# Work on a finished memory and rounding of the next x: placed behind the last key tile of a segment instead of ahead of and in the key tiles

## The chip, the cores and the metric

One core of one Trainium2 chip. The time is the device time of one execution, in microseconds (us). Before the change it was 1409.4 us, the median of 3 runs (1407.93 to 1409.66).

## What is computed

Two attention layers over the same shapes (2048 tokens, width 576, 32 heads of 18), whose outputs are concatenated. A is attention with one key and value head for all query heads. B works in four segments of 512 tokens: causal attention within a segment, mixed by a gate with what the queries read from a memory that the segments ahead have filled:

```python
phi = lambda t: jnp.where(t > 0, t + 1.0, jnp.exp(t))
...
for s in range(N):
    qs, ks, vs = q[:, :, s], k[:, :, s], v[:, :, s]
    logits = jnp.einsum("bhqd,bhkd->bhqk", qs, ks) * scale + mask
    p = _softmax(logits, axis=-1)
    a_dot = jnp.einsum("bhqk,bhkd->bhqd", p, vs)
    pq = phi(qs)
    num = jnp.einsum("bhld,bhde->bhle", pq, M)
    den = jnp.einsum("bhld,bhd->bhl", pq, z)[..., None] + 1e-6
    a_mem = num / den
    o = g * a_mem + (1.0 - g) * a_dot
    outs.append(o)
    pk = phi(ks)
    M = M + jnp.einsum("bhld,bhle->bhde", pk, vs)
    z = z + jnp.einsum("bhld->bhd", pk)
```

Everything is float32. The kernel reaches that accuracy by splitting each operand into a rounded high part and a low part, so that one product becomes three.

## The kernel before

The program has two halves. The first, to about 286 us, projects the inputs: A in four chunks, then B segment by segment (`for s in range(NSEG)`). Then every engine reads a flag and branches on it (L627, L628), and behind the branch comes the attention phase with its own order of work, which the change does not touch.

**A segment of B** goes through these stages, in the order of the code:

- *Five key tiles* (`for t in range(5)`, L449 to L477). TensorE computes the tile of the projection into `pj` (14 matmuls, L253). VectorE takes its maximum `kmB` (L459), ScalarE rounds it into the high part of `qp` (L122), VectorE subtracts for the low part (L123), and the DMA queue of SyncE (SP) stores both (L127). Then phi: two steps on ScalarE (L397, L398) and one on VectorE (L400) make `kf` (in the fifth tile `qf`). With the next tile TensorE transposes `kf` (`natural`, L427) and VectorE copies the result to `pkN` (L428).
- *The next x.* In segments 1 and 2, each key tile also calls `nx[2](t)` (L468), that is `load_xk`: a DMA on SP brings a slice of the next segment's x into `xr`, which has three buffers (L196), VectorE rounds it to `xh` (L209) and subtracts for `xl` (L215, L217). In segment 0 this is called in the query tiles instead.
- *`from_memory(4)`* (L479). For segments 1 and 2 (`LATE_ASK`) it only stores `qf` (L438), and the memory is asked in the attention phase; for segment 3 it multiplies with `Mst` on TensorE at once.
- *Values and keys of the last head.* `values(i, 0)` (L503) for four blocks of tokens, each followed by a copy to `vch` (L505) and a store to `vB` from ScalarE's DMA queue (L508). The transposes of `kn` (L519) give VectorE the maximum `km31` (L522; it stands as `km` in the rows). It is multiplied with `sely` on TensorE (L533) into the PSUM bank `mm`, of which there is one. Then `values(i, 1)`.
- *Four query tiles* (L539 to L551), the bound `pu` on the logits, its store `shB` (L571), and in segment 3 the flag (L412) and then `values(i, 1)`.
- *The memory.* In segments 0 to 2 TensorE adds up phi(k) times v into `pm`, again in the bank `mm` (L586 to L598). VectorE masks it with `bands` (L601), adds it to `Mbd` (L608), copies seven pieces into `Mst` (L613), reduces `zc` (L614) and spreads it over `zst` (L616, five tiles). For segments 0 and 1 two DMAs store `Mst` and `zst` to `mzB` (L618, L619).

In segment 0, most of these operations are pinned: they keep the order of the code. In the other segments a scheduler orders each engine's instructions by when their operands are expected, so the order on an engine is not that of the code. `tc.issue_after(ins)` makes what is issued within it stand behind the instruction `ins` on that engine.

Of the kernel before, what the change touches and what calls it, by code (L numbers as in the profile page):

```python
# [14 lines left out]
ALU = mybir.AluOpType  # L15
AX = mybir.AxisListType
# [10 lines left out]
RT = [18 * h for h in HT]  # L27
H0 = [0, 7, 14, 21, 28]
FIRST = [(0, 1, 3, 4), (0, 1, 1)]
# [7 lines left out]
VW = DH + 1  # L37
# [24 lines left out]
LATE_ASK, ASK = (1, 2), 20  # L62
# [13 lines left out]
def attention_pair_kernel(ctx, tc, a_xT, a_w, a_wo, b_xT, b_w, b_wo, b_beta, ident_d, hmask_d, bmask_d, cmask_d, sel_d, zmask_d, selx_d, sely_d, out):  # L76
    nc = tc.nc
# [26 lines left out]
    mzB = dram("mzB", [128, len(LATE_ASK), 5, MZ], F32)  # L104
# [52 lines left out]
    with ExitStack() as ph:  # L157
# [18 lines left out]
        zmask = pw.tile([128, 5, 32], F32, name="zmask")  # L176
# [87 lines left out]
        for c in range(NCH):  # L264
            ready = {}
            if c == 0:
# [8 lines left out]
                nx = next_x(a_xT, 1)  # L275
# [18 lines left out]
            else:  # L294
                xh, xl = nx[:2]
                nx = next_x(a_xT, c + 1) if c < NCH - 1 else next_x(b_xT, 0)
                if c == 2:
                    wBl, wBh = (pw.tile([128, 5, 3 * D], F32R, name=n) for n in ("wBl", "wBh"))
            for t in TILES:
# [8 lines left out]
                R = RT[t]  # L308
# [22 lines left out]
                i = 5 * (c - 2) + TILES.index(t)  # L331
# [31 lines left out]
        for t in range(5):  # L363
            R = RT[t]
# [14 lines left out]
        Mbd = p2.tile([128, 5, 3, VW], F32, name="Mbd")  # L379
        mx = p2.tile([128, 5, 3, VW], F32, name="mx")  # L380
        Mst = p2.tile([128, 5, 7, DH], F32, name="Mst")
        zst = p2.tile([128, 5, 32], F32, name="zst")
        nc.gpsimd.memset(Mbd, 0.0)
        nc.gpsimd.memset(mx, 0.0)
        bands = p2.tile([128, 2, 3, VW], F32, name="bands")
# [8 lines left out]
        def phi(src, R, nm, bufs, hold=lambda ins: ins):  # L394

            e = p2.tile([128, C], F32, name="ph_e", bufs=2)
            hold(nc.scalar.activation(e[:R], src, AF.Relu, scale=-1.0))  # L397
            hold(nc.scalar.activation(e[:R], e[:R], AF.Exp, scale=-1.0))  # L398
            f = p2.tile([128, C], F32, name=nm, bufs=bufs)
            hold(nc.vector.scalar_tensor_tensor(f[:R], src, 0.0, e[:R], op0=ALU.max, op1=ALU.add))  # L400
            return f

        def loose_flag():
# [7 lines left out]
            nc.vector.tensor_scalar(fm2[:, 1:2], fm2[:, 0:1], float(BOUND_OK), None, op0=ALU.is_gt)  # L411
            nc.vector.tensor_copy(flag, fm2[:, 1:2])  # L412

        for s in range(NSEG):
            xh, xl = nx[:2]
            last = s == NSEG - 1
# [18 lines left out]
            def from_memory(t):  # L435
                R = RT[t]
                if s in LATE_ASK:
                    nc.sync.dma_start(qfB[s][:R, t], fs[t][:R])  # L438
                    return
                pn = ps.tile([128, C], F32, name="mm", bufs=1)  # L440
                nc.tensor.matmul(
                    pn[:R], Mst[:R, t].rearrange("p h d -> p (h d)")[:, :R], fs[t][:R], start=True, stop=True
                )
                nm = p2.tile([128, C], F32, name="nm", bufs=2)
                nc.vector.tensor_scalar(nm[:R], pn[:R], gt[:R, t : t + 1], None, op0=ALU.mult)
                nc.sync.dma_start(numB[s][126 * t : 126 * t + R], nm[:R])


            for t in range(5):  # L449
                if s == t == 0:  # L450
                    pj = ahead
                else:
                    pj = ps.tile([128, C], F32, name="pj", bufs=4)
                    proj(pj[:126], wBh, wBl, xh, xl, 630 + 126 * t if t < 4 else 504, 126)
                if t and not last:
                    natural(f, pkN[:, t - 1, :, 0:126], 0, 126)

                hold = pin if s == 0 else lambda ins: ins
                hold(nc.vector.tensor_reduce(kmB[:126, t : t + 1], pj[:126], axis=AX.X, op=ALU.max, apply_absolute_value=True))  # L459
                qp = split2(pt, pj[:126], 126, hold)  # L460
                if t < 4:
                    store_parts(qp, 0, 126, kB[s], 7 * t, 7)
                    hold(nc.vector.tensor_scalar(kbB[:126, t], zmask[:126, t], kmB[:126, t : t + 1], None, op0=ALU.mult))
                else:
                    store_parts(qp, 0, 72, qB[s], 28, 4)
                    store_parts(qp, 72, 54, kB[s], 28, 3)
                    magnitude(4, pj)
                if s and not last:  # L468
                    nx[2](t)
                if not last or t == 4:  # L470
                    f = phi(pj[:126], 126, "kf" if t < 4 else "qf", 2 if t < 4 else 5, hold)
                    if t == 4:
                        fs[4] = f
                if s == 0:
                    split_wpart(10 + t)
                    if t < 4:
                        load_wpart(11 + t)  # L477
            if s:
                from_memory(4)  # L479
            if s == 0:  # L480
                nc.vector.memset(gt, 0.0)
                for t, lo, hi, n in [(t, H0[t], H0[t] + HT[t], DH) for t in range(5)] + [(5, 0, 28, 4), (6, 28, 32, 32)]:
# [10 lines left out]
            def values(i, hf):  # L493
                pj = ps.tile([128, C], F32, name="pj", bufs=4)
                ops = []
                tk = slice(128 * i, 128 * i + 128)
                n = 288 if hf else 306
                vc = slice(1440, 1728) if hf else slice(1134, 1440)
                for k in range(4):
                    ops += [(xh[:, k, tk], wBh[:, k, vc]), (xl[:, k, tk], wBh[:, k, vc]), (xh[:, k, tk], wBl[:, k, vc])]  # L500
                ops += [(xh[:, 4, tk], wBh[:, 4, vc]), (xh[:, 4, tk], wBl[:, 4, vc])]
                for m, (x, w) in enumerate(ops):
                    nc.tensor.matmul(pj[:, :n], x, w, start=m == 0, stop=m == len(ops) - 1)  # L503
                hs = slice(16 * hf, 16 * hf + 16)
                nc.scalar.copy(vch[:, i, hs, 1:VW], pj[:, :288].rearrange("p (h d) -> p h d", d=DH))  # L505
                if not hf:
                    nc.scalar.copy(kn[:, i], pj[:, 288:306])
                nc.scalar.dma_start(  # L508
                    vB[s][128 * i : 128 * i + 128, 304 * hf : 304 * hf + 304], vch[:, i, hs].rearrange("p h d -> p (h d)")
                )  # L510

            values(0, 0)
            if not last:
                natural(fs[4], pkN[:, 4, :, 0:54], 72, 126)
            for i in range(1, 4):
                values(i, 0)
            tr = ps.tile([128, 4, 128], F32, name="tr", bufs=1)
            for i in range(4):
                nc.tensor.transpose(tr[:DH, i], kn[:, i], ident)  # L519
# [15 lines left out]
            if not last:  # L535
                for i in range(4):
                    values(i, 1)

            for t in range(4):  # L539
                pj = ps.tile([128, C], F32, name="pj", bufs=4)  # L540
# [44 lines left out]
            if s < NSEG - 1:  # L585
                pm = ps.tile([128, C], F32, name="mm", bufs=1)[:, : 5 * 3 * VW].rearrange("p (t m) -> p t m", t=5)  # L586
                for t in range(5):
                    for i in range(4):
                        for g in range(4 if t < 4 else 3):
                            rows = slice(32 * g, min(32 * g + 32, RT[t]))  # L590
                            h = H0[t] + FIRST[t == 4][g]
                            nc.tensor.matmul(
                                pm[rows, t],
                                pkN[:, t, i, rows],
                                vch[:, i, h : h + 3, :].rearrange("p h d -> p (h d)"),
                                start=i == 0,
                                stop=i == 3,
                            )  # L598
                new = mx if s else Mbd
                for n, (R, ts) in enumerate(((126, slice(0, 4)), (72, slice(4, 5)))):  # L600
                    nc.vector.tensor_tensor(  # L601
                        new[:R, ts].rearrange("p t h d -> p t (h d)"),
                        pm[:R, ts],
                        bands[:R, n : n + 1].rearrange("p t h d -> p t (h d)").to_broadcast([R, ts.stop - ts.start, 3 * VW]),
                        op=ALU.mult,
                    )
                if s:
                    nc.vector.tensor_tensor(Mbd[:126], Mbd[:126], mx[:126], op=ALU.add)  # L608
                for ts in (slice(0, 4), slice(4, 5)):
                    for g in range(4 if ts.start < 4 else 3):  # L610
                        rows = slice(32 * g, min(32 * g + 32, RT[ts.start]))
                        w = FIRST[ts.start == 4][g]
                        nc.vector.tensor_copy(Mst[rows, ts, w : w + 3], Mbd[rows, ts, :, 1:VW])  # L613
                nc.vector.tensor_reduce(zc[:126], Mbd[:126, :, :, 0], axis=AX.X, op=ALU.add)  # L614
                for t in range(5):
                    nc.vector.tensor_scalar(zst[: RT[t], t], zmask[: RT[t], t], zc[: RT[t], t : t + 1], None, op0=ALU.mult)  # L616
                if s + 1 in LATE_ASK:
                    nc.sync.dma_start(mzB[:, s, :, :126], Mst.rearrange("p t h d -> p t (h d)"))  # L618
                    nc.sync.dma_start(mzB[:, s, :, 126:], zst)  # L619
            if s == 0:  # L620
                pin(nc.scalar.activation(gt, gt, AF.Exp, scale=-1.0))
                pin(nc.vector.tensor_scalar(gt, gt, 1.0, None, op0=ALU.add))
# [677 lines left out]
```

## Time and profile before

| | |
|---|---|
| Median of 3 runs | 1409.4 us |
| The profiled execution | 1409.26 us, its span 1407.5 us |
| Busy: TensorE (PE), ScalarE (ACT), VectorE (DVE), GpSimd (POOL) | 98%, 85%, 74%, 17% of the span |
| Granted clock of TensorE, mean | 0.995 |
| The four segments of B and the branch | about 118 to 288 us |

A row of a timeline has the start and the duration in us, the engine, the line, the operation, out<-in and the shape; in brackets stands how long the engine was idle ahead of it and what ended that. The letter q behind an engine (SPq, ACTq) marks what its queue does itself: issuing a DMA, a wait, a branch. VectorE's operations overlap a little at their ends, so how long one holds the engine is read from one start to the next.

### The profile page before, as it was taken

What the parts mean: (1) busy time and instruction counts of PE and PEld (TensorE: products, weight loads), DVE (VectorE), ACT (ScalarE), POOL (GpSimd) and SP (SyncE); (2) the same over time, 40 slices, a digit from 0 to 9 for tenths busy, and PEclk for the clock granted to TensorE, in tenths of its full rate; (3) what the DMA queues carried; (4) which work ended last, traced back from release to release, by engine and by line L of the source; (5) the groups of instructions that cost most, each with busy time, mean ns of one, the idle gap of its engine ahead of it and who ended that gap; (6) DMA issues with size and microseconds to landing.
All of it is one profiled execution on the core that took longest, in us unless ns stands there. A gap on an engine that the chain in (4) does not pass through costs nothing.

```text
span 1407.5 us, 41225 instructions
## 1 busy us (share of the span) xinstructions
PE 1386.2 (98%) x17468; PEld 837.5 (60%) x17468; DVE 1045.7 (74%) x1544; ACT 1198.8 (85%) x1479; POOL 234.4 (17%) x335
## 2 busy tenths in 40 slices
PE   9999999989999999999999999999999999999998
PEld 6787888745544555555555555555555555555558
DVE  6656456467787778777878878776879778887883
ACT  4543434479999999999999999999999999999991
POOL 2441000003302310402110122113010220001002
PEclk9999999989999999999999999999999999999999
DMA  9866546567575445332312442333103321120022
GB/s 282 259 213 188 169 149 214 184 177 218 145 215 165 118 137 176 98 119 85 112 58 71 146 144 60 94 106 91 51 33 94 109 75 44 32 67 18 18 69 103
DMA packets 90726, 172.70 MB, mean 123 GB/s; under 512 B 14576, under 2 KB 22889, under 8 KB 90110
## 3 DMA queue, kind: packets, MB, share of 16 engines
q1 hardware_dynamic: 84122, 160.01, 37.0%
q0 software_dynamic: 1664, 4.78, 1.3%
q10 hardware_dynamic: 4752, 5.24, 1.1%
q8 instruction: 138, 2.26, 0.7%
q14 instruction: 50, 0.41, 0.1%
HBM read 99.32 MB, written 70.67 MB: 121 GB/s over the span
## 4 chain that ended last, share of the span: by engine, by line
PE 71%; ACT 4%; DVE 2%; issue 1%; DMA 1%; POOL 0%; SPq 0%; ACTq 0%
PE O L991 33%; PE E L943 21%; PE F L796 11%; ACT P L961 4%; PE E L951 3%; PE E L1201 2%; DVE W L958 1%; PE F L852 1%; DMA vseg<-vB 0%; DMA woA<-a_wo 0%; DVE sm L747 0%; PE F L1201 0%; PE O L1201 0%; DVE o L857 0%; DVE oe L1000 0%
## 5 line engine op out<-in xcount | busy, mean ns | idle before, releaser
L961 ACT ACTIVATE P<-E 128x1024 f32<-128x1024 f32 (+1 forms) x800 | 789.4, 1079 | 4.8 <-PE E L943 4.6
L958 DVE COPY W<-E 128x1024 f32<-128x1024 f32 (+2 forms) x416 | 453.7, 1091 | 142.5 <-PE E L943 83.6
L991 PE MATMUL O<-P,VA 128*32 128x256 f32 x7504 | 508.1, 380 | 0.0
L961 ACT ACTIVATE P<-W 128x1024 f32<-128x1024 f32 (+1 forms) x330 | 370.7, 1123 | 6.9 <-DVE W L958 6.5
L991 PEld LDWEIGHTS O<-P,VA 128*32 128x32 f32 x7504 | 259.0, 110 | 139.1 <-issue 6.4
L943 PE MATMUL E<-stA,kstA 56*128 56x512 f32 x1920 | 317.0, 430 | 2.8 <-DVE W L958 1.9
L943 PEld LDWEIGHTS E<-stA,kstA 56*128 56x128 f32 x1920 | 154.6, 184 | 160.4 <-issue 93.0
L966 POOL TENSOR_SCALAR_AFFINE_SELECT P<-P 128x256 f32<-128x256 f32 (+1 forms) x192 | 95.0, 495 | 418.6 <-ACT P L961 380.6
L780 POOL TENSOR_TENSOR o<-o,rb 126x512 f32<-126x512 f32 (+1 forms) x55 | 72.8, 1350 | 488.6 <-DVE PD L926 328.9
L796 PE MATMUL F<-woB,o 126*32 126x192 f32 (+1 forms) x1920 | 126.6, 338 | 0.0
L991 PE MATMUL O<-PD,VA 128*32 128x256 f32 x688 | 88.9, 379 | 0.0
L796 PEld LDWEIGHTS F<-woB,o 126*32 126x32 f32 (+1 forms) x1920 | 38.6, 108 | 74.5 <-issue 68.7
L991 PE MATMUL O<-P,vseg 128*32 128x256 f32 (+2 forms) x1536 | 81.5, 344 | 0.1
L919 DVE TENSOR_SCALAR PD<-E 128x512 uint32<-128x512 f32 x86 | 59.4, 691 | 28.0 <-PE E L943 26.4
L1000 DVE COPY oe<-O 128x512 f32<-128x512 f32 x64 | 44.3, 692 | 41.7 <-PE O L991 40.8
L253 PE MATMUL pj<-xh,wBh 128*126 128x512 f32 x180 | 72.1, 401 | 0.0
L253 PE MATMUL pj<-xh,wBl 128*126 128x512 f32 x180 | 71.6, 398 | 0.0
L122 ACT CAST qp<-pj 126x512 fp32r<-126x512 f32 (+1 forms) x54 | 30.9, 584 | 44.2 <-DVE kmB L459 26.5
L123 DVE TENSOR_TENSOR qp<-pj,qp 126x512 fp32r<-126x512 f32 (+1 forms) x54 | 36.8, 686 | 39.5 <-ACT qp L122 39.3
L796 PE MATMUL F<-woA,o 126*32 126x192 f32 (+1 forms) x960 | 63.9, 338 | 0.0
L951 PE MATMUL E<-stB 56*128 56x256 f32 (+3 forms) x512 | 61.5, 347 | 2.1 <-ACT P L961 1.3
L991 PEld LDWEIGHTS O<-P,vseg 128*32 128x32 f32 x1536 | 48.8, 109 | 24.5 <-issue 1.9
(198 smaller groups left out, 1571.7 us busy)
## 6 DMA issues: line engine op xcount, KB each, us to landing
stB<-kB SPq DMA_DIRECT2D x96, 144.0 KB
stB<-qB SPq DMA_DIRECT2D x32, 288.0 KB
stA<-qA SPq DMA_DIRECT2D x30, 288.0 KB
oA<-oe SPq DMA_DIRECT2D x32, 256.0 KB
oB<-oe SPq DMA_DIRECT2D x32, 256.0 KB
qA<-qp SPq DMA_DIRECT2D x16, 504.0 KB
kB<-qp SPq DMA_DIRECT2D x16, 504.0 KB
qB<-qp SPq DMA_DIRECT2D x16, 504.0 KB
```

The source lines that it names most:

```text
L123: hold(nc.vector.tensor_tensor(qp[:R, 1, :n], src, qp[:R, 0, :n].bitcast(F32), op=ALU.subtract))
L253: nc.tensor.matmul(dst, w[:, c0 : c0 + M], x, start=i == 0, stop=i == len(ops) - 1)
L780: ins = tc.keep_in_program_order(nc.gpsimd.tensor_tensor(dst, a, b, op=op))
L796: nc.tensor.matmul(dst[32 * j : 32 * j + 32], parts[ab, c][: RT[t], t, r0 : r0 + 32], wo[ab][: RT[t], t, c0 : c0 + n], start=start, stop=stop,
L919: v.tensor_scalar(y, e, EXP_A, EXP_B, op0=ALU.mult, op1=ALU.add)
L943: nc.tensor.matmul(e[:, j], kstA[rows, 128 * kt : 128 * kt + 128], st[rows, h, :], start=True, stop=True)
L951: nc.tensor.matmul(e[:, j, c0 : c0 + 512 - 128 * k], st[rows, 4 + h, ks], st[rows, h, 128 * k :], start=True, stop=True)
L958: gate.append(nc.vector.tensor_copy(src[:, hs, :n], e[:, hs, :n]))
L961: nc.scalar.activation(p[:, hs, :n], src[:, hs, :n], AF.Exp, scale=SCALE)
L966: nc.gpsimd.affine_select(diag, diag, pattern=[[0, 2], [0, m], [1, 128]], base=0, channel_multiplier=-1, compare_op=ALU.is_ge, fill=0.0)
L991: nc.tensor.matmul(o[32 * j : 32 * j + 32, q0 : q0 + n], v, p[:, j % 2, p0 : p0 + n], start=m == hf == 0, stop=last and hf == 1,)
L1000: nc.vector.tensor_copy(osb, o)
```

## The change

The VectorE work on a finished memory (L601 to L619) becomes a function `collect`, which is called in the next segment, behind its five key tiles and after the last phi on VectorE. `from_memory(4)` moves behind the values of the first half. The calls that round the next x leave the key tiles: three stand among `values(1..3, 0)`, two among `values(0..1, 1)`.

```diff
-            hold(nc.vector.scalar_tensor_tensor(f[:R], src, 0.0, e[:R], op0=ALU.max, op1=ALU.add))
+            summed[:] = [hold(nc.vector.scalar_tensor_tensor(f[:R], src, 0.0, e[:R], op0=ALU.max, op1=ALU.add))]
             return f
...
+        rest, summed = [], []
         for s in range(NSEG):
...
-                if s and not last:
-                    nx[2](t)
                 if not last or t == 4:
...
             if s:
-                from_memory(4)
+                with tc.issue_after(summed[0].ins):
+                    rest.pop()()
...
             for i in range(1, 4):
+                if s and not last:
+                    nx[2](i - 1)
                 values(i, 0)
+            if s:
+                from_memory(4)
             tr = ps.tile([128, 4, 128], F32, name="tr", bufs=1)
...
                 for i in range(4):
                     values(i, 1)
+                    if s and i < 2:
+                        nx[2](3 + i)
...
-                new = mx if s else Mbd
...
+                def collect(s=s, pm=pm):
+                    new = mx if s else Mbd
...
+                    if s + 1 in LATE_ASK:
+                        nc.sync.dma_start(mzB[:, s, :, :126], Mst.rearrange("p t h d -> p t (h d)"))
+                        nc.sync.dma_start(mzB[:, s, :, 126:], zst)
+
+                rest.append(collect)
```

What the scheduler makes of it, at three places. First VectorE at the first key tile of segment 1, before (line numbers behind L400 shift by up to 9 between the two programs):

```order
L135 TENSOR_TENSOR shp<-sht,shp 128x512
L601 TENSOR_TENSOR Mbd<-mm,bands 126x228
L601 TENSOR_TENSOR Mbd<-mm,bands 72x57
L613 COPY Mst<-Mbd 32x4x54 x3
L613 COPY Mst<-Mbd 30x4x54
L613 COPY Mst<-Mbd 32x54 x2
L613 COPY Mst<-Mbd 8x54
L614 TENSOR_REDUCE zc<-Mbd 126x5
L459 TENSOR_REDUCE kmB<-pj 126x1
L616 TENSOR_SCALAR zst<-zmask,zc 126x32 x4
L616 TENSOR_SCALAR zst<-zmask,zc 72x32
```

and the same place now:

```order
L135 TENSOR_TENSOR shp<-sht,shp 128x512
L631 TENSOR_SCALAR gt<-gt 128x7
L209 CAST xh<-xr 128x512
L632 RECIPROCAL gt<-gt 128x7
L215 TENSOR_TENSOR xl<-xr,xh 128x512
L633 TENSOR_SCALAR omg<-gt 128x7
L209 CAST xh<-xr 128x512
L460 TENSOR_REDUCE kmB<-pj 126x1
L215 TENSOR_TENSOR xl<-xr,xh 128x512
L464 TENSOR_SCALAR kbB<-zmask,kmB 126x32
L123 TENSOR_TENSOR qp<-pj,qp 126x512
L209 CAST xh<-xr 128x512
```

The work on the memory has left this place, and the rounding of the next x (L209, L215), which stood behind the tile's `qp` before, now stands ahead of and behind `kmB`. In segment 2 it is the same: of L134, L135 and the rows between them and `kmB`, L601, L608, L613 and L614 have gone, and a cast and a subtraction of x more stand there, with one more cast right behind `kmB`.

Second, VectorE in segment 2 from the last phi to the maximum over `kn`, before:

```order
L400 SCALAR_TENSOR_TENSOR qf<-pj,ph_e 126x512
L209 CAST xh<-xr 128x512
L215 TENSOR_TENSOR xl<-xr,xh 128x512
L428 COPY pkN<-tr 128x4x54
L522 TENSOR_REDUCE km_2257<-tr 18x1
L534 TENSOR_SCALAR kbB<-zmask,mm 72x32
```

and now:

```order
L400 SCALAR_TENSOR_TENSOR qf<-pj,ph_e 126x512
L608 TENSOR_TENSOR mx<-mm,bands 126x228
L608 TENSOR_TENSOR mx<-mm,bands 72x57
L615 TENSOR_TENSOR Mbd<-Mbd,mx 126x285
L429 COPY pkN<-tr 128x4x54
L620 COPY Mst<-Mbd 32x4x54 x3
L620 COPY Mst<-Mbd 30x4x54
L620 COPY Mst<-Mbd 32x54 x2
L620 COPY Mst<-Mbd 8x54
L621 TENSOR_REDUCE zc<-Mbd 126x5
L526 TENSOR_REDUCE km_2248<-tr 18x1
```

The work on the memory stands here, ahead of the maximum `km`, and the rounding of the next x that stood here has gone. On TensorE, the matmul that reads `km` stands two matmuls later than before, and the transposes of the segment's first `kf` four matmuls earlier.

Third, ScalarE at the end of segment 3, where the last values are copied and stored and the flag is read, before:

```order
L505 COPY vch<-pj 128x16x18
L508 DMA vB_76<-vch 128x304
L505 COPY vch<-pj 128x16x18
L508 DMA vB_76<-vch 128x304
L505 COPY vch<-pj 128x16x18
L627 TENSOR_LOAD flag
L628 COMPARE_AND_BRANCH
```

and now:

```order
L505 COPY vch<-pj 128x16x18
L508 DMA vB_76<-vch 128x304
L505 COPY vch<-pj 128x16x18
L508 DMA vB_76<-vch 128x304
L636 TENSOR_LOAD flag
L637 COMPARE_AND_BRANCH
```

The DMA of the last values stood behind the branch and stands ahead of it now. In segment 3, TensorE's matmuls with `Mst` stand up to 12 matmuls later. Behind the branch the order of no engine differs.

More of the change, by code (lines that the diff above doesn't have):

```diff
@@ L598, in attention_pair_kernel @@
                             )
-                new = mx if s else Mbd
[L600 to L619, printed above, removed]
+                def collect(s=s, pm=pm):
+                    new = mx if s else Mbd
+                    for n, (R, ts) in enumerate(((126, slice(0, 4)), (72, slice(4, 5)))):
+                        nc.vector.tensor_tensor(
+                            new[:R, ts].rearrange("p t h d -> p t (h d)"),
+                            pm[:R, ts],
+                            bands[:R, n : n + 1].rearrange("p t h d -> p t (h d)").to_broadcast([R, ts.stop - ts.start, 3 * VW]),
+                            op=ALU.mult,
+                        )
+                    if s:
+                        nc.vector.tensor_tensor(Mbd[:126], Mbd[:126], mx[:126], op=ALU.add)
+                    for ts in (slice(0, 4), slice(4, 5)):
+                        for g in range(4 if ts.start < 4 else 3):
+                            rows = slice(32 * g, min(32 * g + 32, RT[ts.start]))
+                            w = FIRST[ts.start == 4][g]
+                            nc.vector.tensor_copy(Mst[rows, ts, w : w + 3], Mbd[rows, ts, :, 1:VW])
+                    nc.vector.tensor_reduce(zc[:126], Mbd[:126, :, :, 0], axis=AX.X, op=ALU.add)
+                    for t in range(5):
+                        nc.vector.tensor_scalar(zst[: RT[t], t], zmask[: RT[t], t], zc[: RT[t], t : t + 1], None, op0=ALU.mult)
+                    if s + 1 in LATE_ASK:
+                        nc.sync.dma_start(mzB[:, s, :, :126], Mst.rearrange("p t h d -> p t (h d)"))
+                        nc.sync.dma_start(mzB[:, s, :, 126:], zst)
```

## The prediction

> **What bounds the kernel now.** I read four views in this order: the page's busy times and chain, a table of stretches, TensorE's timeline through the segments, and then VectorE's, ScalarE's and the DMA queue's rows around each idle time of TensorE. First the page (busy us and share of the span for each engine, then the chain that ended last), and the stretches (start and end, length, busy time of each engine, granted clock, DMA share, GB/s):
>
> ```profile
> PE 1386.2 (98%) x17468; PEld 837.5 (60%) x17468; DVE 1045.7 (74%) x1544; ACT 1198.8 (85%) x1479; POOL 234.4 (17%) x335
> PE 71%; ACT 4%; DVE 2%; issue 1%; DMA 1%; POOL 0%; SPq 0%; ACTq 0%
> 118.00:286.00 168.00, 165.12 (x1304) 136.35 (x1303) 93.09 (x205) 65.66 (x137) 1.05 (x3) 1.00 0.59 188
> 286.16:287.73 1.57, 0.00 (x0) 0.03 (x1) 0.00 (x0) 0.40 (x1) 0.00 (x0) 1.00 0.05 14
> ```
>
> TensorE is busy for 98% of the span and carries 71% of the chain. VectorE's 74% is therefore no measure of what lighter VectorE work is worth: only where TensorE waits for VectorE can this change give time back. The four segments of B's part that it touches lie in the stretch 118 to 286, and there TensorE is idle for 168.00 − 165.12 = 2.88 us in all. Its timeline (start, duration, engine, line, operation; in brackets the idle time before it and what ended it) shows where:
>
> ```profile
> 137.80 0.62 PE L427 MATMUL tr<-ident,kf 126*128 126x126 f32 x4 [1.77 <-DVE kf L400]
> 190.49 0.65 PE L427 MATMUL tr<-ident,kf 126*128 126x126 f32 x4 [0.97 <-DVE kf L400]
> 287.73 1.12 PE L943 MATMUL E<-st,kstA 56*128 56x512 f32 x4 [1.57 <-SPq L628]
> ```
>
> Twice, at the first key tile of segments 1 and 2, the transposes of `kf` wait for VectorE: 1.77 + 0.97 = 2.74 us, or 0.19% of the run. That is all that a lighter VectorE can win. The third wait, 1.57 us, is the branch on the flag behind segment 3. The order of the attention phase behind the branch is the same before and after on every engine, so the whole effect lies ahead of and at the branch. A measurement of this kernel can tell about 0.2% (2.8 us) from no change.
>
> **Segment 1, first key tile.** VectorE's rows before:
>
> ```profile
> 130.69 0.51 DVE L601 TENSOR_TENSOR Mbd<-mm,bands 126x228 f32<-126x228 f32 x2
> 131.54 1.74 DVE L613 COPY Mst<-Mbd 32x216 f32<-32x216 f32 x7 [0.34 <-DVE Mbd L601]
> 133.41 0.68 DVE L459 TENSOR_REDUCE kmB<-pj 126x1 f32<-126x512 f32 x1
> 134.00 0.81 DVE L616 TENSOR_SCALAR zst<-zmask,zc 126x32 f32<-126x32 f32 x5
> 135.71 0.75 DVE L209 CAST xh<-xr 128x512 fp32r<-128x512 f32 x2
> 136.38 0.68 DVE L215 TENSOR_TENSOR xl<-xr,xh 128x512 fp32r<-128x512 f32 x1
> 136.98 0.68 DVE L400 SCALAR_TENSOR_TENSOR kf<-pj,ph_e 126x512 f32<-126x512 f32 x1
> ```
>
> From starts to starts, an operation of 512 columns holds VectorE 0.6 us (133.41 to 134.00) and a cast 0.34 (135.71 to 136.38, two). The work on the memory stands ahead of the maximum `kmB` and takes 133.41 − 130.69 = 2.72 us; from `kmB` to the end of `kf` it is 136.98 + 0.68 − 133.41 = 4.25 us. The change takes the 2.72 us away. But the rounding of the next x does not leave the key tiles: in the order as built, two casts, a subtraction and three tiny operations on the gate have moved up ahead of `kmB`. They cost 2 × 0.34 + 0.6 + about 0.35 = 1.6 us, so `kmB` starts at 132.3 instead of 133.4 and **1.1 us** is won, if the second cast finds its x. That x is loaded by the first of these two DMAs; the other rows show how long such a load takes (issue on the DMA queue, then the cast that uses it):
>
> ```profile
> 128.68 1.75 SPq L196 DMA_DIRECT2D xr<-b_xT  x2
> 217.44 0.37 SPq L196 DMA_DIRECT2D xr<-b_xT  x1
> 222.28 0.42 DVE L209 CAST xh<-xr 128x512 fp32r<-128x512 f32 x1
> 56.38 1.24 SPq L196 DMA_DIRECT2D xr<-b_xT  x2
> 64.30 0.43 DVE L209 CAST xh<-xr 128x512 fp32r<-128x512 f32 x1 [2.15 <-DMA xr<-b_xT]
> ```
>
> At 222.28 the x was there without a wait, so its load took at most 4.8 us; at 64.30 the cast waited for a load issued 7.9 us before, in the busiest stretch. The cast is now due at 128.68 + 3.25. I take 3.6 us for the load, an estimate between a quiet transfer (1.84 us at most, a row further down) and the 4.8 us: a stall of 0.35, **−0.75 us** in all. The ends are −1.1 (in time) and +0.5 (4.8 us). What is moved behind the last key tile is covered:
>
> ```profile
> 152.64 0.62 PE L427 MATMUL tr<-ident,qf 126*128 126x126 f32 x4
> 156.70 0.27 PE L519 MATMUL tr<-ident,kn 128*18 128x128 f32 x1
> ```
>
> The last `qf` was done by 152.64; 2.72 us and five small operations (0.7) later it is 156.1, and the next that TensorE needs of VectorE, the maximum over `kn`, can't start before 156.97. Without that 0.9 us of cover the work would cost what it overhangs. The two stores to `mzB` go with it; the stores queued behind them on the DMA queue are read only in the attention phase. No instruction of POOL or of its queue is moved.
>
> **Segment 2, first key tile.** VectorE's rows before, and TensorE's last matmul ahead of its wait:
>
> ```profile
> 181.33 0.42 DVE L134 CAST shp<-sht 128x512 fp32r<-128x512 f32 x1
> 183.66 0.68 DVE L215 TENSOR_TENSOR xl<-xr,xh 128x512 fp32r<-128x512 f32 x1
> 184.26 1.73 DVE L613 COPY Mst<-Mbd 32x216 f32<-32x216 f32 x7
> 186.13 0.68 DVE L459 TENSOR_REDUCE kmB<-pj 126x1 f32<-126x512 f32 x1
> 188.21 0.42 DVE L209 CAST xh<-xr 128x512 fp32r<-128x512 f32 x1
> 189.75 0.68 DVE L400 SCALAR_TENSOR_TENSOR kf<-pj,ph_e 126x512 f32<-126x512 f32 x1
> 189.12 0.39 PE L253 MATMUL pj<-xl,wBh 128*126 128x512 f32 x1
> ```
>
> After, two casts (L134 and one of x) and four operations of 512 columns stand between 181.33 and `kmB`: 2 × 0.34 + 4 × 0.6 = 3.1 us, `kmB` at 184.4 instead of 186.1. Right behind it stands another cast of x, and the load of that x can only be issued when a subtraction has freed one of the three `xr` buffers, at 181.33 + 0.34 + 0.6 + 0.1 = 182.4. With 3.6 us for the load it lands at 186.0, while VectorE comes to the cast at 185.0: a stall of 1.0 us, with the first `kf` queued behind it. Walking on (cast, subtraction, low part, next `kmB`, then the two exponential steps on ScalarE) `kf` ends at 189.75, and the transposes could start at 189.85. But in TensorE's order they now stand 4 matmuls earlier (4 × 0.23 us), so TensorE comes there at 188.6: a wait of 1.27 us instead of 0.97, **+0.3 us**. With the x in time it would wait 0.3 (−0.7); with 4.8 us of load, 2.5 (+1.5).
>
> **Segment 2, maximum over kn.** Before, VectorE is idle when the transposes of `kn` arrive:
>
> ```profile
> 221.68 0.68 DVE L400 SCALAR_TENSOR_TENSOR qf<-pj,ph_e 126x512 f32<-126x512 f32 x1
> 222.50 0.62 PE L427 MATMUL tr<-ident,qf 126*128 126x126 f32 x4
> 224.52 0.68 DVE L522 TENSOR_REDUCE km<-tr 18x1 f32<-18x512 f32 x1 [0.81 <-PE tr L519]
> 225.33 0.28 PE L533 MATMUL mm<-km,sely 18*72 18x1 f32 x2
> ```
>
> After, the seven copies into `Mst` (1.77 us) and the reduction to `zc` come between. The last `qf` ends on VectorE at 222.3; two products, a sum, the copy of `pkN`, which waits until 223.35 for its transposes (one place later than the 222.50 of before), the seven copies and `zc` bring the reduction to 225.5 and its end to 226.2. TensorE comes to the matmul on `km` two matmuls later than before, at 225.85. **+0.4 us**, from nothing (if the copies come up earlier) to 0.8. In segment 3 the work on the last memory likewise stands behind the last `qf`, with the matmuls that read `Mst` 12 places later: +0.1, from 0 to 0.3, for in the order TensorE still has 31 matmuls of values to run.
>
> **The branch.** ScalarE's and the DMA queues' rows:
>
> ```profile
> 284.76 0.33 ACTq L508 DMA_DIRECT2D vB<-vch  x1
> 286.20 0.40 ACT L505 COPY vch<-pj 128x288 f32<-128x288 f32 x1 [1.47 <-PE pj L503]
> 287.43 0.33 ACTq L508 DMA_DIRECT2D vB<-vch  x1
> L628 SPq EVENT_SEMAPHORE  x8: 17/17/17, 287.0 to 287.5; - x8
> 203.69 0.33 ACTq L508 DMA_DIRECT2D vB<-vch  x1
> 205.53 0.38 SPq L619 DMA_DIRECT2D mzB<-zst  x1
> SPq L619 <- DMA vB<-vch: 13.7, 1, 13.7
> ```
>
> The SyncE side of the branch waits on eight semaphores, those of the DMA queues, between 287.0 and 287.5, and TensorE starts at 287.73. Before, the last of the value stores stood behind the branch (issued at 287.43), so the last to be waited for was the one issued at 284.76, done by 287.0: 2.24 us at most. Now the last store stands ahead of the branch. Its copy still ends at 286.60, it is issued at 286.63, and it has to land first. A store of the same kind on quiet queues took at most 205.53 − 203.69 = 1.84 us (in the last row the second store waits for the first). So it lands between 288.47 and 288.87, and the rest of the eight and the start of TensorE follow in 0.43 to 0.73 us: 288.9 to 289.6. That is +1.2 to +1.85; I take **+1.5 us**, the middle, since both rows are of this very store. TensorE is idle in all that time, as the row of the stretch 286.16 to 287.73 shows (0.00 busy), and nothing hides it.
>
> The Trainium skill, "DMA: Bandwidth & Descriptors", section "Anatomy of one DMA — SWDGE (gpsimd) path", gives a fixed part of about 2.0 us, mostly the receipt of the write, and bytes over 436 GB/s, for another kind of queue; for this store of 156 KB that is an estimate of 2.36 us. By it the branch would cost 1.7 to 2.0 us and the sum would be 0.3 us higher. The trace's 1.84 is below it, so I keep the rows.
>
> **The sum** is made against the profiled execution, 1409.26 us (span 1407.5), which is 0.14 us under the median of 1409.4: −0.75 + 0.3 + 0.4 + 0.1 + 1.5 = +1.55, so **1410.8 us**.
>
> **The rivals.**
> - *The branch costs nothing* (chance 0.12): the last store may be covered by another wait of the eight, or the branch may not look at that queue. For it speaks that the eight semaphores take 0.5 us whatever is late. Against it, the last store comes 1.87 us behind the third. With both x in time: 1409.26 − 1.1 − 0.7 + 0.4 = 1407.9 us.
> - *Slower: the hoisted rounding stands in front of the key tile and waits for late x* (0.15). The place is the cast ahead of `kmB` in segment 1 and the cast behind it in segment 2. It decides from a load of more than 3.25 us and 2.6 us, and each tenth beyond is lost in full. Its price is a stall as at 64.30, 2.15 us, in each, in place of the 0.35 and 1.0 us of the forecast: (2.15 − 1.1) + (2.15 − 0.7) + 0.4 + 0.1 + 1.5 = +4.5, 1413.8 us. For it: the load of segment 2 is issued together with `shB` and the loads of `kstA`. Against it: only two casts of x waited in the whole run, both in the stage before.
> - *The change does not do what it says* (counted with the forecast): for the rounding this is already so in the order, and in the forecast. Were VectorE's gain nothing as well, it would be 1409.26 + 0.4 + 0.1 + 1.5 = 1411.3, within the forecast.
> - *The longer idle time at the branch costs clock* (0.12). The last rows:
>
> ```profile
> 288.50:289.00 0.50, 0.35 (x3) 0.00 (x0) 0.00 (x0) 0.36 (x1) 0.00 (x0) 0.70 0.52 172
> 289.00:298.00 9.00, 7.29 (x40) 3.37 (x41) 6.99 (x10) 7.75 (x9) 0.22 (x1) 0.50 0.51 118
> 298.00:299.00 1.00, 1.00 (x6) 0.34 (x4) 0.23 (x1) 0.65 (x1) 0.00 (x0) 0.53 0.63 145
> ```
>
> The granted clock is half from about 288.7 to 298.9, 10.2 us behind an idle time of 1.57. With 3.1 us idle it may stay low a third longer: 3.4 us at half speed lose 1.7, 1412.5 us. The Trainium skill, "TensorE: Matmul & The Clock Gate", section "Part 1: The HAM clock gate", tells of a free-running window of about 3.4 us, after an idle one of which the clock is halved, until a busy one. The 10.2 us are three such windows, which agrees; the halving after only 1.57 us of full idleness does not fit its wording closely.
>
> **How the numbers follow.** The forecast has 0.61. Its own terms reach from −1.1 − 0.7 + 0 + 0 + 1.2 = −0.6 to 0.5 + 1.5 + 0.8 + 0.3 + 1.85 = +4.95, with all five at one end, 1408.7 to 1414.2. The range that leaves out no more than 2 in 10 goes down to the first rival, with 0.3 us for the spread of the runs (1407.93 to 1409.66 before), and up to the second: 1407.6 to 1413.8. Faster by over 0.2% means below 1406.6, which is below every case (the whole 2.74 us would give 1406.5): 0.04. Slower by over 0.2% means above 1412.2: the second rival, half of the clock's, and the upper tail of the forecast, 0.22. Within: 0.74.
>
> **What would show it.** Right: TensorE's wait at the first `kf` of segment 1 falls from 1.77 to about 1.0; that of segment 2 stays between 0.3 and 2.5, released by VectorE behind a cast that itself waits for a DMA; a new wait of about 0.4 at the matmul on `km` of segment 2; the store of values issued before the branch, and the wait there about 3.1 us. Wrong: a wait at the branch still of 1.6 (first rival), idle time of 2 us at the casts (second), half clock for some 14 us (clock), or a difference of time within the attention phase, which I take as unchanged.

## The result and the profile after

The changed kernel takes 1414.17 us (median of 7 runs, 1411.61 to 1415.2) against 1408.68 before: a ratio of 1.0031, 95% interval 1.0022 to 1.0041. Run once more as an experiment, beside others, it took 1411.64 us (11 runs) against 1408.65: 1.0021, interval 1.0012 to 1.0030. By these ratios it is slower by 4.4 and 3.0 us, where 1.5 was forecast. The first medians are 5.5 us apart: four of the seven runs took 1414.2 to 1415.2 us and three 1411.6 to 1412.3, which is where the second measurement lies. The direction is the forecast one, but the size is two to three times as large, and beyond the 0.2% to which the forecast gave most of its chance. The second measurement lies well inside the range. The first lies at its upper end of 1413.8: 1.0031 times the 1409.26 from which the sum was made is 1413.6, and the median itself, 1414.17, is 0.4 above it. The profiled run took 1414.61 us, its span is 1412.9.

First the places at which the prediction expected something, on TensorE (idle time ahead and its cause in brackets):

```profile
139.33 0.62 PE L428 MATMUL tr<-ident,kf 126*128 126x126 f32 x4 [1.17 <-DVE kbB L464]
191.45 0.65 PE L428 MATMUL tr<-ident,kf 126*128 126x126 f32 x4 [1.25 <-DVE kf L400]
225.74 0.28 PE L537 MATMUL mm<-km,sely 18*72 18x1 f32 x2 [0.22 <-DVE km L526]
293.90 1.85 PE L952 MATMUL E<-st,kstA 56*128 56x512 f32 x6 [4.91 <-SPq L637]
```

The wait at the first `kf` of segment 1 fell from 1.77 to 1.17 us, that of segment 2 rose from 0.97 to 1.25, the matmul on `km` waits newly for 0.22, and the wait at the branch rose from 1.57 to 4.91 us. The first two are close to the forecast (1.0, 1.27), the third is half of it (0.4); the fourth is not (3.1).

VectorE at the first key tiles of segments 1 and 2 shows why the gain is so small:

```profile
132.90 0.42 DVE L209 CAST xh<-xr 128x512 fp32r<-128x512 f32 x1
133.35 0.69 DVE L215 TENSOR_TENSOR xl<-xr,xh 128x512 fp32r<-128x512 f32 x1
134.51 0.43 DVE L209 CAST xh<-xr 128x512 fp32r<-128x512 f32 x1 [0.38 <-DMA xr<-b_xT]
134.85 0.68 DVE L460 TENSOR_REDUCE kmB<-pj 126x1 f32<-126x512 f32 x1
187.60 0.43 DVE L209 CAST xh<-xr 128x512 fp32r<-128x512 f32 x1 [0.79 <-DMA xr<-b_xT]
```

The rounding of the next x stands ahead of `kmB`, and VectorE, which waited for no load here before, waits for that of x: 0.38 us in segment 1 (forecast 0.35) and 0.79 in segment 2 (forecast 1.0).

To add up, the program is cut at five marks of TensorE's timeline: the start of the last memory matmul of segments 0, 1 and 2, the end of the last matmul of values, and the first matmul of the attention phase. us:

| run | segment 1 | segment 2 | segment 3 | wait at the branch | attention to the end |
|---|---|---|---|---|---|
| before | 52.82 | 51.76 | 54.29 | 1.57 | 1119.8 |
| changed, first profile | 52.27 | 52.61 | 54.68 | 4.91 | 1119.0 |
| changed, second profile | 52.00 | 52.54 | 54.69 | 4.20 | 1118.8 |

From the first profile: −0.55 + 0.85 + 0.39 + 3.34 − 0.8 = +3.2 us. Its span is 5.4 longer; the other 2.1 lie ahead of segment 1, nearly all in code that is the same. Of them 1.9 arise in the first 10 us:

```profile
6.13 1.17 PE L285 MATMUL pj<-xh,wAh 128*114 128x512 f32 x4 [0.58 <-DVE wAh L226]
```

```profile
6.57 2.02 PE L285 MATMUL pj<-xh,wAh 128*114 128x512 f32 x4 [1.00 <-DVE wAh L226]
```

The first row is of before, the second of the changed kernel: the same four matmuls took 1.17 and 2.02 us. The granted clock was full from 5.4 us on in the one run and from 10.2 in the other, and in the second profile of the changed kernel from 7.5. So about 1.4 us of this single run are the lower clock at its start, and 0.4 the longer wait in front of that row. The second profile, only 0.2 us late at segment 1, is the better witness: −0.82 + 0.78 + 0.40 + 2.63 − 0.95 + 0.2 = +2.2 us against the span of before.

### The profile page after: what moved, and what is told of

It reads as the page before. It is cut to its first block, busy times and chain, and to the rows that moved or that the text cites. A ratio compares the mean times of both kernels' runs of the same rounds, so it can differ in the third digit from the quotient of the medians.

```text
span 1412.9 us, 41220 instructions
## 1 busy us (share of the span) xinstructions
PE 1388.8 (98%) x17468; PEld 838.8 (59%) x17468; DVE 1044.5 (74%) x1544; ACT 1198.7 (85%) x1479; POOL 233.4 (17%) x335
## 4 chain that ended last, share of the span: by engine, by line
PE 70%; ACT 4%; DVE 2%; DMA 2%; issue 1%; SPq 0%; POOL 0%; ACTq 0%
PE O L1000 32%; PE E L952 20%; PE F L805 11%; ACT P L970 4%; PE E L960 3%; PE E L1210 2%; PE F L861 1%; DVE W L967 1%; DMA oB<-oe 1%; DMA vseg<-vB 0%; DVE sm L756 0%; DMA o<-oB 0%; DMA woA<-a_wo 0%; PE F L1210 0%; PE O L1210 0%
```

## The experiments

**Theory 1**: the loss is the wait at the branch, because the last store of values now stands ahead of ScalarE's read of the flag. **Theory 2**: it is the moved VectorE work itself, which delays segments 2 and 3. The first two kernels move one instruction each.

**The last store ahead of the flag, all else as before.** `stored` holds the last DMA to `vB`:

```diff
-    loose = nc.values_load(flag[0:1, 0:1], min_val=0, max_val=1)
+    with tc.issue_after(stored[0].ins):
+        loose = nc.values_load(flag[0:1, 0:1], min_val=0, max_val=1)
```

> The kernel before, with one instruction moved: ScalarE's last store of values stands ahead of its read of the flag instead of behind the branch; nothing else differs on any engine. Theory 1 (the store that the branch waits for is the larger part of the loss): the wait of TensorE at the branch rises from 1.57 us to between 3.1 and 4.9, and the time by 1.5 to 3.4 us (0.1 to 0.24%), the waits at the two first kf stay. Theory 2 (the loss is the moved VectorE work and TensorE's changed order in segments 2 and 3): no change within 0.5 us.

Measured: 1410.81 us (11 runs) against 1408.81, ratio 1.0015 (1.0006 to 1.0024). The segments are those of before to 0.2 us (52.81, 51.56, 54.29). TensorE's waits and the last store in the timeline, then the eight semaphores on SyncE (duration in ns, first and last start):

```profile
137.39 0.62 PE L428 MATMUL tr<-ident,kf 126*128 126x126 f32 x4 [1.78 <-DVE kf L400]
290.20 1.95 PE L945 MATMUL E<-st,kstA 56*128 56x512 f32 x6 [4.66 <-SPq L630]
286.00 0.33 ACTq L509 DMA_DIRECT2D vB<-vch  x1
```

```profile
L630 SPq EVENT_SEMAPHORE  x8: 17/17/17, 286.3 to 290.1; - x8
```

One store, issued as soon as its copy ends, costs 3.1 us at the branch. It accounts for the whole wait; theory 2 expected none of it. The time rises by 2.0 us, which is two thirds of the 3.0 that the changed kernel loses in its second measurement. But in the prediction the store was to cost 1.5, and it took from 286.00 to 289.60 to land, 3.6 us, not 2.2.

**The changed kernel, its last store on GpSimd's software queue**, which SyncE's side of the branch does not wait for:

```diff
-                nc.scalar.dma_start(
+                (nc.gpsimd if last and (i, hf) == (3, 1) else nc.scalar).dma_start(
```

> The changed kernel, with one instruction moved: the last store of values is issued on GpSimd's software queue, whose semaphores SyncE's side of the branch does not wait for. Theory 1: the wait of TensorE at the branch falls from 4.9 to about 1.6 us, and the time to about 0.7 us over before (0 to 1.5), that is 2 to 4 us under the changed kernel. Theory 2: the wait may fall, but the time stays 3 us or more over before.

Measured: 1409.5 us against 1408.81, ratio 1.0002 (0.9993 to 1.0011). No loss can be told from the spread any more, with segments 2 and 3 as long as in the changed kernel (52.73, 54.66). The wait fell to 2.66 us, not to 1.6: the third store, issued at 287.35, landed only at 290.68. The store `shB`, issued in front of it at 286.08, is about 1 us nearer to the branch than before, since the flag comes later in segment 3; that this is the cause was not tried by itself. The fetch described below is not: it runs from 290.02 to 291.30, and the last packets of this store pass in its first 0.2 us.

**One half of the change alone.** First the memory work alone, with `nx[2](t)` called in the key tiles again:

> The changed kernel with the rounding of the next x called in the key tiles as before; only the work on the memory and the store of the last query part stay moved. The engines' orders differ from the changed kernel in a few rows late in segment 2 only. Theory 1 (the store at the branch, which comes with the moved memory work): as the changed kernel, 2.5 to 5.5 us over before, wait at the branch 4 to 5 us. Theory 2, in the form that the moved calls of the rounding cost: within 1 us of before.

Measured: 1411.67 us against 1408.65, ratio 1.0020 (1.0011 to 1.0029), wait at the branch 4.68, segments 51.97, 52.82 and 54.72. This is the changed kernel in every part, to 0.3 us. Then the calls of the rounding alone:

> The kernel before with the calls of the rounding moved as in the change, and nothing else. In the order the work on the memory still stands ahead of the first kmB, and the last store of values stands behind the branch. Theory 1: within 1 us of before, waits of about 1.8 and 1.0 us at the two first kf and 1.6 at the branch. Theory 2: 2 us or more over before.

Measured: 1408.95 us, ratio 1.0003 (0.9994 to 1.0012), waits of 1.79 us at the first `kf` and 1.56 at the branch. So the half of the change that was to move the rounding does nothing that can be measured: the scheduler, which orders by readiness, puts it where VectorE has room, and it was the departure of the memory work that drew it ahead of `kmB`.

**The changed kernel again**, beside these two:

> The changed kernel once more, beside the others on one chip. Theory 1: 3 to 5 us over before, wait at the branch 4 to 5 us with a 16 KB fetch of instructions in it, of some 1.6 us, ahead of the last 8 rows of the last store. If that fetch is a chance of one profile, the wait is 3.1 us.

Measured: 1411.64 us, ratio 1.0021 (1.0012 to 1.0030), wait at the branch 4.20. The fetch of instructions that the expectation speaks of is there again: 1.03 us long, ahead of the end of the last store.

**What makes the store so late.** In the first profile of the changed kernel, the DMA traffic of two stretches, 290.2 to 292.2 and 291.4 to 293.3 (busy tenths of the 16 DMA engines in 40 slices; then, for each queue, packets, MB and share of the 16 engines). Queue q10 is ScalarE's, q8 fetches instructions:

```profile
DMA  0069989998632000000000000000000000010010
...
q10 hardware_dynamic: 141, 0.15, 22.6%
q8 instruction: 1, 0.02, 5.1%
```

```profile
DMA  0000000000001001020010010000000000000000
...
q10 hardware_dynamic: 9, 0.01, 2.8%
```

The store's packets pass by 290.9, and then one fetch of 16 KB holds one DMA engine: 5.1% of 16 engines over 2 us are 1.6 us. Only then do the last nine packets of the store come, eight rows of 1216 bytes and the signal, one after the other as from a single engine. (The profile does not name a packet's engine; that they share one is read from the times.) In the trace the fetch runs from 290.36 to 292.00 and the first of the nine starts at 291.99; in the experiment with one store moved, from 286.80 to 288.29 and at 288.28. In the other three profiles with the last store ahead of the branch on ScalarE's queue, and without the added matmuls that follow, the first of the nine starts within 0.02 us of the fetch's end, too. Fifteen of the store's sixteen signals were there at 291.41 (287.78), the last at 293.30 (289.60). The fetch starts 1.0 to 1.5 us behind TensorE's own branch in every profile; before, it ran at 287.40, when no store was waited for any more. The Trainium skill, "Runtime: NRT & Kernel Launch", section "Instruction fetch mechanics", has it that instructions come by DMA in pieces of 16 KiB and that a branch can force such a fetch; the size and the place agree.

If the fetch is the cause, later matmuls should make it faster. Ten unused matmuls of 128x288 (1.34 us) ahead of TensorE's read of the flag push the branch, and so the fetch, back:

```diff
+                if last and (i, hf) == (3, 1):
+                    pad = ps.tile([128, C], F32, name="mm", bufs=1)
+                    with tc.issue_after(end.ins):
+                        for m in range(10):
+                            padded[:] = [nc.tensor.matmul(pad[:, :n], *ops[m], start=m == 0, stop=m == 9)]
```

> The changed kernel with 10 more matmuls of 128x288 (1.3 us, their result is not used) on TensorE between the last values and its read of the flag; nothing else differs. Theory F (the 16 KB fetch of instructions, which starts 1.0 to 1.4 us behind TensorE's branch, holds one DMA engine and that engine's rows of the last store): the fetch moves 1.3 us back, the store lands whole within 2.3 us of its issue, and SyncE passes the branch 1 to 1.8 us earlier after that issue than in the changed kernel, so TensorE's idle time behind its last matmul falls from 4.2 to 4.9 to about 1.5 to 2 us and the time is 0.5 to 1.5 us under the changed kernel, in spite of more work. Theory S (the store takes 2.9 to 3.9 us by itself): the first matmul of the attention phase comes as long after the store's issue as before, and the time stays.

> The kernel before with the last store ahead of the flag (as in the first experiment) and the same 10 matmuls of 128x288 ahead of TensorE's read of the flag. Theory F: TensorE's idle time falls from 4.66 to about 1.5 to 2 us, and the first matmul of the attention phase comes 1 to 1.8 us earlier after the store's issue than in the first experiment; the time is 0.5 to 1.5 us under that one. Theory S: it comes as long after the store's issue as there, and the time stays.

Measured, on the kernel before with its store ahead of the flag:

```profile
286.46 0.33 ACTq L514 DMA_DIRECT2D vB<-vch  x1
289.09 1.27 PE L950 MATMUL E<-st,kstA 56*128 56x512 f32 x6 [1.77 <-SPq L635]
```

From the store's issue to the first matmul of the attention phase it is 2.63 us, where it was 290.20 − 286.00 = 4.20: 1.57 us less with 1.34 us more work. The store landed 2.03 us after its issue, and the fetch (288.96) came behind it. Idle time and added matmuls together are 3.11 us, 1.54 over the 1.57 of before. The time is 1409.43 us, ratio 1.0010 (1.0001 to 1.0019), against 1.0015 without the matmuls. On the changed kernel the same took the wait from 4.20 to 2.42 us, not to the expected 1.5 to 2, and the time to 1410.55, ratio 1.0014 (1.0005 to 1.0023) against 1.0021. The traces show theory F; the times lean its way, but their intervals overlap. In the padded changed kernel the store still took 2.7 us. An earlier fetch of 16 KB ran there from 284.04 to 285.28, and the last signal of the stores under way came 0.4 to 2.1 us after their others, as if one DMA engine were behind; that it was this fetch was not tried.

**The rounding really held behind the last phi**, as the change says:

```diff
                 if s and not last:
-                    nx[2](i - 1)
+                    with tc.issue_after(summed[0].ins):
+                        nx[2](i - 1)
...
                     if s and i < 2:
-                        nx[2](3 + i)
+                        with tc.issue_after(summed[0].ins):
+                            nx[2](3 + i)
```

> The changed kernel, with the rounding of the next x also issued behind the last phi of the key tiles (as the work on the memory is), so that it really leaves them. Theory 1: both waits of TensorE at the first kf are gone (up to 2.7 us), the loads of x are early enough, and the store at the branch still costs 1.5 to 3.4: the time is between 1.5 us under and 1.5 us over before. Theory 2: what stands behind the last phi delays the maximum over kn, the query tiles and the Mst matmuls further, new waits of over 1 us there, and the time is 4 us or more over before.

Measured: 1412.87 us, ratio 1.0026 (1.0016 to 1.0037). Theory 1 was wrong here, and theory 2 right. Both waits at the first `kf` are gone and segment 1 takes 50.94 us, but segment 2 takes 53.83 and segment 3 55.47. In segment 2 (VectorE's cast, then TensorE):

```profile
227.82 0.43 DVE L209 CAST xh<-xr 128x512 fp32r<-128x512 f32 x1 [2.48 <-DMA xr<-b_xT]
230.01 0.39 PE L574 MATMUL nd<-aq,kbB 126*32 126x512 bf16 x2 [2.31 <-ACT aq L434]
```

The cast of x waits for its load in front of the query tiles' work, as the second rival had it, only later in the segment, and behind it TensorE waits 2.31 us for ScalarE. The granted clock then is half from 230.86 to 234.27, across the end of segment 2, which it is at this place in no kernel without the long wait; TensorE is busy all that time, so about 1.7 us more are lost (an estimate: half of 3.41). With the last store on GpSimd's queue as well:

> The rounding held behind the last phi and the last store of values on GpSimd's software queue, together. Theory 1: 1 to 2.5 us under before (about 1406.5 to 1408), with no wait of TensorE at a first kf and about 1.6 us at the branch. Theory 2: still slower than before.

Measured: 1408.8 us, ratio 0.9999 (0.9990 to 1.0008); segments 50.97, 53.88 and 55.88, 2.67 at the branch. So neither theory came true: it is neither faster nor slower. Segment 1 wins 1.85 us, segments 2 and 3 lose 3.7 and the branch 1.1; in the profile, most of this comes back behind the branch, where the phase takes 1117.4 us instead of 1119.8 and the half clock lasts 6.83 us instead of 10.24. That part is not a gain that the placement was shown to bring.

**Placed by segment.** Before the change, VectorE is idle in segment 2 between the third and the fourth key tile (from 200 to 216 us it has one operation). So the last kernel holds both pieces of work behind the last phi in segment 1 and behind the third tile's in segment 2, and leaves the memory work ahead of segment 3, and segment 3's `from_memory(4)`, where they were (the lines for the latter are left out here):

```diff
+                    if t == (2 if s == 2 else 4):
+                        anchor[:] = summed
...
-            if s:
-                with tc.issue_after(summed[0].ins):
+            if rest:
+                with tc.issue_after(anchor[0].ins):
                     rest.pop()()
...
-                rest.append(collect)
+                if s == 2:
+                    collect()
+                else:
+                    rest.append(collect)
```

with `anchor` in place of `summed` for the rounding, too.

> Work on the memory and rounding held behind the last phi in segment 1, behind the phi of the third key tile in segment 2 (where VectorE idles 7 us before the fourth), and the memory work ahead of segment 3 as before; in the order the last store of values stands behind the branch again. Theory 1: both waits at the first kf gone, no new one over 0.6 us, 1.6 us at the branch: 1.5 to 2.7 us under before (1406 to 1407.5). Theory 2 (what stands behind a phi always meets another wait of the same size): within 1 us of before or slower.

Measured: 1405.9 us (11 runs, 1404.94 to 1407.05) against 1408.65, ratio 0.9981 (0.9972 to 0.9990): faster than both kernels. Busy times of the stretch 118 to 283, and the first matmul of the attention phase:

```profile
118.00:283.00 165.00, 164.69 (x1302) 135.95 (x1301) 95.13 (x205) 65.74 (x137) 1.06 (x3) 1.00 0.60 191
```

```profile
284.92 0.92 PE L961 MATMUL E<-st,kstA 56*128 56x512 f32 x4 [1.51 <-SPq L646]
```

TensorE is idle for 0.31 us of that stretch, where it was 2.88 before. The segments take 50.97, 50.91 and 54.54 us, 2.45 less than before in all: nearly the 2.74 that the prediction called the most that a lighter VectorE can win. The time fell by 2.75 us, with an interval of 1.4 to 3.9, so it is chance that 2.75 and 2.74 agree this closely. The last store stands behind the branch again, without having been put there.

## Why the prediction was right and wrong

- **What bounds the kernel**: right. TensorE's two waits are all there is to win in the segments, 2.74 us; the last experiment takes 2.45 of it there.
- **Segment 1**, −0.75 forecast, −0.55 and −0.82 measured. The step from the order of the instructions (the rounding does not leave the key tiles but moves up ahead of `kmB`) and the late load, 3.6 us, were right: it took 3.69 us here (issued at 130.82) and 3.63 in segment 2 (at 183.97), and the stall is 0.38 for the 0.35 forecast.
- **Segment 2**, +0.3 at the first `kf` and +0.4 at `km`: the waits show +0.28 and +0.22, the whole segment +0.85 and +0.78. The sum of 0.7 is near, but in part by luck: the wait at `km` is half as long as forecast, and one that the forecast did not have makes up for it, for ScalarE in the query tiles (0.24 in the second profile):

```profile
232.63 0.39 PE L572 MATMUL nd<-aq,kbB 126*32 126x512 bf16 x2 [0.23 <-ACT aq L434]
```

  The remaining 0.1 us is busy time of TensorE.
- **Segment 3**, +0.1 forecast, +0.4 measured. No new wait of TensorE over 0.3 us shows there; its small matmuls stand in another order and hold it longer. Why was not settled.
- **The branch**: the step that failed in size. "+1.2 to +1.85; I take +1.5 us" was the right mechanism, shown by moving that one instruction both ways, but the wait rose by 3.34 and 2.63 us. The landing was taken from two earlier stores (1.84 and 2.24 us), during which no fetch of 16 KB ran (in the second, one of 8 KB took 0.31 us); behind the branch, a fetch of 1.0 to 1.6 us goes through one of the same DMA engines, and one engine's rows are enough to hold the signal. Without it (the padded kernel before) the store lands in 2.03 us, and the 1.54 us found there are the 1.5 of the forecast. The wait passed the +1.85 that the forecast gave as its bound. That the time still fell inside the range, or at its edge, is luck in part: the range reached to 1413.8 for the sake of late loads, which were not what cost the time.
- **The attention phase** was taken as unchanged, and gave back 0.79 and 0.95 us. Before, TensorE starts on it and stops again at once:

```profile
289.81 1.65 PE L943 MATMUL E<-st,kstA 56*128 56x512 f32 x6 [0.96 <-issue]
```

  "issue" is a wait for nothing that the profile shows. It is there after the waits of 1.51 to 1.57 us at the branch (0.96 to 1.55 us in three profiles) and, with 0.45, after one of 2.66; it is absent after all waits of 4.2 us or more, but also after 2.67 and in the two padded kernels (1.77 and 2.42). So a long wait at the branch seems to hide this one; what TensorE waits for here was not settled. The phase also depends on how much of the half clock lies in it: over all twelve profiles it takes 1117.4 to 1119.8 us, and before is the longest of them.
- **The rivals**: "the branch costs nothing" fell with the first experiment. The late loads were real, but at 0.38 and 0.79 us instead of 2.15 each; with the rounding held further back they came to 2.48. The clock did not stay low for longer: half for 10.2 us again (293.5 to 303.8), in part within the wait, where it costs nothing.

```profile
293.50:294.00 0.50, 0.10 (x1) 0.13 (x1) 0.00 (x0) 0.00 (x0) 0.14 (x1) 0.54 0.00 0
294.00:303.00 9.00, 8.33 (x44) 3.77 (x44) 6.90 (x10) 8.06 (x9) 0.00 (x0) 0.50 0.44 98
303.00:304.00 1.00, 1.00 (x7) 0.75 (x6) 0.00 (x0) 0.25 (x2) 0.00 (x0) 0.61 0.72 154
```

## What to carry to other kernels

Where a scheduler decides the order, read what a moved call does to every queue, to the end of the program part: here one store that slipped from behind a branch to ahead of it cost 3.1 us at the branch and 2.0 us of the time, where the edit could have won 2.74 at the most. Ahead of a branch that waits for all DMAs of the hardware queues, as this one does, the last DMA to land sets the time, and it shares its engines with the fetch of the code behind the branch. And place moved work by where its engine idles in that segment, not by one rule for all: the same work at three anchors, with what the scheduler made of the rest, gave +3.0, +4.1 and −2.75 us.

## What the hardware showed unexpectedly

- A 16 KB fetch of instructions near the branch took 0.92 to 1.65 us, and a store of 152 KB that gives sixteen signals is done when the last of them comes: 15 of 16 signals came within 2 us of the issue, the sixteenth after 3.6 and 3.8 us.
- The half clock behind the branch came in lengths of 10.24 us (six profiles) or 6.83 (six), and a stretch of 3.41 us began late in segment 2 of the two kernels with the rounding held, 0.9 and 1.3 us behind a wait of TensorE of 2.31 and 2.79 us: multiples of 3.41. It set in anywhere from 2.3 us ahead of the first matmul of the phase to 2.8 us after it.
- The twelve profiles show the full granted clock only from 4.2 to 10.5 us after the start, which made about 1.4 us between two of the profiles; a profile of one run has to be cleared of that before its sum is compared.
